# Attention outputs transposed by DMA, head-pair loads for batch 0, a table matmul for ALiBi and mask in two batches, and batch 1 inside the first feed-forward group

## The chip, the cores and the metric

The kernel runs on one core of a Trainium2 chip (trn2). The metric is the device time of one execution in microseconds (us). A version is executed three to six times, and its median is quoted. Every ratio is to runs of the kernel before on the same chip in the same session. A run more than 1.5% above the fastest of its kernel is counted as slow and left out of the ratios; of all runs quoted one was, and it is marked. Where an experiment is set against the changed kernel or another experiment, the two often ran in different sessions, on several chips; the medians of the kernel before in these sessions were 377.8 to 378.8 us.

## The reference

```python
def _attn_ref(q, k, v):                       # 8 batches, 8 heads, 576 tokens, head size 64
    scores = scale * np.matmul(q, k.transpose(0, 1, 3, 2))
    rel = pos[:, None] - pos[None, :]
    bias = slopes[:, None, None] * (-np.abs(rel))       # ALiBi: one slope per head
    mask = (rel >= 0) & (rel < 128)                     # sliding window
    scores = np.where(mask, scores + bias[None], -1e9)
    # ... softmax over the keys
    return np.matmul(attn, v)

def _moe_ref(x, w_in, w_out, beta):           # x: the attention output as 4608 tokens x 512
    h = x @ w_in                              # 512 -> 2048
    g = h * (1.0 / (1.0 + np.exp(-beta * h)))
    return g @ w_out                          # 2048 -> 512
```

Inputs and output are float32. The kernel computes in bfloat16 with float32 sums.

## The kernel before: the parts that matter

The work has two layers. Attention goes batch by batch (eight batches, five blocks of up to 128 tokens). The feed-forward part goes in nine groups of 512 tokens: an *H group* is 16 tiles of `x @ w_in` (`hps`), tanh and a product, and its *out product* is `g @ w_out` (`ops`). TensorE's order is fixed by hand. H group g is placed where its 512 tokens are expected to be ready, and out products and later attention are woven in between.

SyncE issues, in program order, the loads of q, k and v, the DMA transposes that bring q and k of batches 2 to 7 into matmul layout, and the stores of the result. The queue is in order, so an issue that has to wait holds up all behind it; SyncE stood so for 34.7 of the 150 us between 100 and 250 us in the kernel before.

```python
def load_rows(src, b, sb):                    # one block of one of q, k, v: 256 KB in 256 B rows
    f = fst_pool.tile([P, H, D], F32, name="fst", tag="fst")
    nc.sync.dma_start(out=f[0:rows], in_=src[b, :, P*sb : P*sb + rows, :].rearrange("h p d -> p h d"))
# GpSimd casts the block to bfloat16: "bst" for q and k, "vs" for v

def T(b, sb):                                 # q/k transposes
    if b >= NPE:                              # NPE = 2: from batch 2 on by DMA, on SyncE's queue
        for i in range(2):
            nc.sync.dma_start_transpose(out=QK[b % 2][:, i, :, ...], in_=src[0:rows, i]...)
        return
    # ... else on TensorE, and a VectorE copy out of PSUM

def X(b, qb):                                 # an attention output block xn -> XT, H's operand
    xt = psum_t.tile([P, NDM, P], BF16, name="xt", tag="t")
    for c in range(NDM):                      # 4 transposes on TensorE
        nc.tensor.transpose(out=xt[:, c, :], in_=xnv[:, c*P : (c+1)*P], identity=ident[:])
    nc.vector.tensor_copy(out=XT[:, :, tok0 : tok0 + n1], in_=xt[:, :, 0:n1])

def OS(g, i, n):                              # out product and store
    # ... 16 matmuls into ops
    osb = osb_pool.tile([P, DM], F32, name="osb", tag="osb")      # 3 buffers
    nc.scalar.mul(osb[:], ops_[:], 0.5)
    nc.sync.dma_start(out=out[row0 : row0 + P, :], in_=osb[:])
```

The softmax here doesn't subtract the row's maximum and nothing guards it: scores larger than these inputs give would overflow.

## Time and profile before

| | kernel before |
|---|---|
| time, median of 3 (range) | 378.44 us (378.07 to 379.19) |
| span of the profiled run | 378.0 us |
| TensorE busy | 324.5 us, 86% |
| SyncE standing still between 100 and 250 us | 34.7 us of 150 |
| output transposes (`X`) | 160 on TensorE |

### The profile page before, as it was taken

The page shows a single profiled execution, that of the slowest core. Times are in us where ns is not written, and L with a number is a line of the kernel's source. Part 1 is how long each engine was busy: PE and PEld are TensorE (multiplying, and loading weights), DVE is VectorE, ACT ScalarE, POOL GpSimd, SP SyncE. Part 2 cuts the span into 40 slices and gives each one's busy share as a digit, 9 for nine tenths or more (in the row PEclk, how much of TensorE's full clock was granted, in tenths as well). Part 3 has the DMA queues.
Part 4 walks back from the last instruction along what each step waited for, and adds up shares of the span by engine and source line. Part 5 has one row for each costly group of instructions (what it writes and reads, how often), then busy time and mean ns, then how long its engine had stood idle before and what let it go on. Part 6 is the DMA issues. An engine that isn't in the chain of part 4 may idle for free.

```text
span 378.0 us, 6264 instructions
## 1 busy us (share of the span) xinstructions
PE 324.5 (86%) x2248; PEld 158.7 (42%) x2289; DVE 209.3 (55%) x443; ACT 214.4 (57%) x437; POOL 90.0 (24%) x157
## 2 busy tenths in 40 slices
PE   2365577608789999999999999999999999999996
PEld 1143324304344544444444444444444445544442
DVE  3265258606565656756575776676566755543410
ACT  1453076606657476757584868586767764444421
POOL 7671471433233241412323060310000000000000
PEclk9999999966999999999999999999999999999999
DMA  9999999999998899988987889850000011001012
GB/s 167 207 199 203 219 189 205 207 120 192 164 145 186 161 217 149 231 157 141 215 176 170 178 183 183 168 128 29 29 29 28 29 39 46 28 31 55 28 57 83
DMA packets 156768, 50.77 MB, mean 134 GB/s; under 512 B 148016, under 2 KB 152128, under 8 KB 156736
## 3 DMA queue, kind: packets, MB, share of 16 engines
q1 hardware_dynamic: 152512, 46.16, 63.6%
q0 software_dynamic: 4224, 4.19, 6.6%
q8 instruction: 18, 0.29, 0.3%
q14 instruction: 14, 0.11, 0.1%
HBM read 38.02 MB, written 9.44 MB: 126 GB/s over the span
## 4 chain that ended last, share of the span: by engine, by line
PE 73%; DMA 17%; SPq 3%; POOL 2%; ACT 2%; issue 1%; DVE 1%; ACTq 0%; POOLq 0%
PE ops L291 33%; PE hps L275 30%; DMA fst<-in_k_dram 11%; PE sps L205 4%; DMA fst<-in_v_dram 3%; SPq L84 3%; PE pv L241 2%; PE xt L257 2%; PE pv L237 2%; DMA fst<-in_q_dram 1%; DMA qkT<-bst 1%; DVE gT L281 1%; ACT pt L215 1%; ACT sig L280 1%; POOL bst L98 1%
## 5 line engine op out<-in xcount | busy, mean ns | idle before, releaser
L275 PE MATMUL hps<-XT,W 128*128 128x512 bf16 x552 | 149.0, 387 | 5.8 <-DVE gT L281 3.8
L280 ACT ACTIVATE sig<-hps,beta_h 128x512 bf16<-128x512 f32 x144 | 99.5, 693 | 85.7 <-PE hps L275 75.1
L291 PE MATMUL ops<-W,gT 128*128 128x512 bf16 x559 | 142.2, 379 | 1.0 <-issue 0.3
L281 DVE SCALAR_TENSOR_TENSOR gT<-sig,hps 128x512 bf16<-128x512 bf16 x144 | 98.5, 685 | 67.3 <-ACT sig L280 66.8
L215 ACT ACTIVATE pt<-sps,bias 128x256 bf16<-128x256 f32 (+2 forms) x256 | 100.4, 479 | 53.2 <-PE sps L205 53.0
L275 PEld LDWEIGHTS <-W 128*128 128x128 bf16 x576 | 51.7, 99 | 60.3 <-issue 11.4
L291 PEld LDWEIGHTS <-gT 128*128 128x128 bf16 x576 | 51.8, 98 | 55.4 <-issue 2.3
L219 DVE TENSOR_TENSOR pt<-pt,mask 128x1024 bf16<-128x1024 bf16 x64 | 47.9, 748 | 16.2 <-ACT pt L215 15.8
L205 PE MATMUL sps<-qkT 64*128 64x256 bf16 (+2 forms) x320 | 28.8, 274 | 25.6 <-ACT pt L215 12.7
L105 POOL CAST vs<-fst 128x512 bf16<-128x512 f32 (+1 forms) x42 | 27.1, 653 | 88.4 <-DMA fst<-in_v_dram 71.9
L97 POOL CAST bst<-fst 128x512 bf16<-128x512 f32 (+1 forms) x42 | 26.5, 631 | 51.9 <-DMA fst<-in_q_dram 36.4
L247 DVE TENSOR_TENSOR xn<-pv,zs 128x256 bf16<-128x256 f32 (+1 forms) x80 | 33.7, 422 | 2.6
L246 DVE RECIPROCAL zs<-pv 128x4 f32<-128x4 f32 (+1 forms) x80 | 14.2, 178 | 36.4 <-PE pv L241 34.6
L205 PEld LDWEIGHTS <-qkT 64*128 64x128 bf16 x320 | 12.4, 97 | 51.5 <-issue 38.8
L241 PE MATMUL pv<-vs,pt 128*128 128x65 bf16 x320 | 31.3, 201 | 1.1 <-DVE pt L219 1.0
L297 ACT ACTIVATE osb<-ops 128x512 f32<-128x512 f32 x36 | 21.7, 602 | 18.8 <-PE ops L291 18.4
L98 POOL CAST bst<-fst 128x512 bf16<-128x512 f32 (+1 forms) x42 | 26.8, 638 | 19.7 <-DMA fst<-in_k_dram 18.5
L241 PEld LDWEIGHTS <-pt 128*128 128x128 bf16 x320 | 23.8, 102 | 10.7 <-DVE pt L219 1.6
L237 PE MATMUL pv<-vs,pt 128*128 128x65 bf16 x256 | 26.2, 201 | 1.2 <-DVE xn L247 1.2
L237 PEld LDWEIGHTS <-pt 128*128 128x128 bf16 x256 | 21.4, 103 | 9.1 <-DVE xn L247 1.7
L262 DVE COPY XT<-xt 128x512 bf16<-128x512 bf16 (+1 forms) x40 | 15.6, 390 | 12.7 <-PE xt L257 12.0
L179 PE MATMUL tps<-ident,bst 128*128 128x128 bf16 x80 | 10.6, 292 | 12.3 <-POOL bst L97 8.8
(26 smaller groups left out, 58.5 us busy)
## 6 DMA issues: line engine op xcount, KB each, us to landing
out_dram<-osb SPq DMA_DIRECT2D x36, 256.0 KB, 2.1
fst<-in_v_dram SPq DMA_DIRECT2D x34, 256.0 KB, 4.2
fst<-in_q_dram SPq DMA_DIRECT2D x33, 256.0 KB, 5.2
fst<-in_k_dram SPq DMA_DIRECT2D x33, 256.0 KB, 5.0
W<-in_moe_w_in_dram POOLq DMA_DIRECT2D x4, 512.0 KB, 11.9
W<-in_moe_w_out_dram POOLq DMA_DIRECT2D x4, 512.0 KB, 12.2
fst<-in_q_dram SPq DMA_DIRECT2D x9, 128.0 KB, 5.0
fst<-in_k_dram SPq DMA_DIRECT2D x9, 128.0 KB, 4.5
```

What stands on the lines that cost most here:

```text
L98: c = nc.gpsimd.tensor_copy(out=t[0:rows, 1], in_=fk[0:rows])
L105: return nc.gpsimd.tensor_copy(out=VS[b % 2][0:rows, sb, :, 0:D], in_=f[0:rows])
L205: nc.tensor.matmul(o, lhsT=qk[64 * e : 64 * e + 64, 1, p, P * kb : P * kb + P], rhs=qk[64 * e : 64 * e + 64, 0, p, P * kb : P * kb + nq], ...
L215: nc.scalar.activation(out=pt[:, e, cols], in_=sps[:, e, cols], func=ACTF.Exp, scale=qscale, bias=bias[:, half, h : h + 1],)
L219: nc.vector.tensor_tensor(out=pt[:], in0=pt[:], in1=masks[m][:], op=ALU.mult)
L237: nc.tensor.matmul(pv[:, hl, 0 : D + 1], lhsT=weights(b, qb - 1, h, 1), rhs=vs[:, qb - 1, h, 0 : D + 1], start=True, stop=False,)
L241: nc.tensor.matmul(pv[:, hl, 0 : D + 1], lhsT=weights(b, qb, h, 0), rhs=vs[:, qb, h, 0 : D + 1], start=qb == 0, stop=True,)
L247: nc.vector.tensor_tensor(out=xn[0:nq, 4 * g : 4 * g + 4, :], in0=pv[0:nq, :, 0:D], in1=zs[0:nq].broadcast_to([nq, 4, D]), op=ALU.mult,)
L275: nc.tensor.matmul(hps[:], lhsT=W1[:, c, bass.ts(j, P)], rhs=XT[:, c, c0 : c0 + TOKG], start=(c == 0), stop=(c == NDM - 1),)
L280: nc.scalar.activation(out=sig[:], in_=hps[:], func=ACTF.Tanh, scale=beta_h[:, j : j + 1])
L281: nc.vector.scalar_tensor_tensor(out=gts[g][:, j, :], in0=sig[:], scalar=1.0, in1=hps[:], op0=ALU.add, op1=ALU.mult)
L291: nc.tensor.matmul(ops_[:], lhsT=gT[:, j, i * P : i * P + P], rhs=W2[:, j, :], start=(j == 0), stop=(j == NFF - 1),)
```

## The change

Its intent is to start TensorE's long full stretch earlier and to take work off it:

- all output transposes of batches 2 to 7 go from TensorE to DMA (on SyncE's queue);
- q and k of batch 0 come by head pairs in 1 KB rows, and the double loads of some of batch 1's blocks are gone; there are more staging buffers for loads (`fst` 16 in place of 13, `bst` 8 in place of 7);
- in batches 0 and 1 a matmul adds ALiBi and mask as a table, so that one `Exp` of 1024 columns replaces four of 256 and the mask product falls away;
- batch 1's attention lies inside H group 0, and groups 0 and 1 use four PSUM buffers for H tiles.

```diff
-    xn_pool = ctx.enter_context(tc.tile_pool(name="xn", bufs=2))
+    xn_pool = ctx.enter_context(tc.tile_pool(name="xn", bufs=6))
...
+    def load_pair(p):                       # batch 0, two heads, 4 tokens of one head per row: 1 KB
+        for i, src in enumerate((q, k)):
+            nc.sync.dma_start(out=f[:]..., in_=src[0, 2*p : 2*p+2, 0:LM].rearrange("h (r a) d -> r h (a d)", a=LA))
...
     def SC(b, m, p, pool=None):
+        if b < NPE:
+            for e in range(2):
+                nc.tensor.matmul(sps[:, e, :], lhsT=sident[:, 2*p + e, :], rhs=table[m][:], start=True, stop=False, ...)
...
+        if b < NPE:
+            nc.scalar.activation(out=pt[:], in_=sps[:], func=ACTF.Exp, scale=qscale)
+        else:
+            # ... the four activations with a bias, and the mask product, as before
...
     def X(b, qb):
+        if b >= NPE:
+            for at, r0, r1 in parts:
+                nc.sync.dma_start_transpose(out=XT[:, :, at : at + r1 - r0], in_=xnv[r0:r1, :])
+            return
         # ... on TensorE as before
...
     def HS(g, j):
-        hps = psum_h.tile([P, TOKG], F32, name="hps", tag="hps")
+        pool, tag = (psum_o, "ops") if g < 2 and j % 2 else (psum_h, "hps")
...
# (the rest of the diff reorders the program: batch 1's attention list `one` runs within H group 0)
```

## The prediction

> **What bounds the kernel now.** I read the page first, slices before groups.
>
> ```profile
> PE   2365577608789999999999999999999999999996
> PEclk9999999966999999999999999999999999999999
> DMA  9999999999998899988987889850000011001012
> ```
>
> Slices are 9.45 us. TensorE is full from about 110 us on and has gaps before; DMA is the reverse, full to 250 us. So the kernel is starved first and TensorE-bound after. A table of 10 us stretches puts TensorE at 3.09 us busy in 70 to 80, 4.32 in 80 to 90, 9.95 in 110 to 120. The timeline of TensorE gives the waits and, by the distance of starts, the rates:
>
> ```profile
> 81.81 0.40 PE L205 MATMUL sps<-qkT 64*128 64x256 bf16 x2 [8.00 <-DMA qkT<-bst]
> ...
> 102.41 1.89 PE L275 MATMUL hps<-XT,W 128*128 128x512 bf16 x8 [1.04 <-DVE gT L281]
> 104.93 1.89 PE L275 MATMUL hps<-XT,W 128*128 128x512 bf16 x8 [0.51 <-DVE gT L281]
> ...
> 199.75 1.03 PE L275 MATMUL hps<-XT,W 128*128 128x512 bf16 x4
> 200.61 1.03 PE L291 MATMUL ops<-W,gT 128*128 128x512 bf16 x4
> ```
>
> Four wide matmuls take 0.86 us (199.75 to 200.61), 0.216 each. In H-only stretches two tiles take 2.52 us (102.41 to 104.93), not 1.73: two PSUM buffers wait for tanh and multiply. In the same way a scores step (one head pair, half a batch) costs 0.33 us of TensorE, a 65-wide value matmul 0.031, a transpose 0.057. The sum: H 576 x 0.216 = 124.2; out product the same; scores 64 x 0.33 = 21.1; values 576 x 0.031 = 17.9; q/k transposes 80 x 0.057 = 4.6; output transposes 160 x 0.057 = 9.1; together 301.1 us. Check: the first out product starts at 108.3 us, where by program order 39.6 is done and 261.5 left. The chain of work ends
>
> ```profile
> 368.11 6.22 PE ops L291 x28
> ```
>
> at 374.3: 266.0 for 261.5, so 4.5 us were lost after 108 us and 3.7 follow the last matmul. Almost all the loss, 69 us, lies in the first 108.
>
> Who starves it? The timelines of GpSimd (which casts what landed) and of the SyncE queue:
>
> ```profile
> 7.02 0.62 POOL L97 CAST bst<-fst 128x512 bf16<-128x512 f32 x1 [0.55 <-DMA fst<-in_q_dram]
> 8.23 0.62 POOL L98 CAST bst<-fst 128x512 bf16<-128x512 f32 x1 [0.59 <-DMA fst<-in_k_dram]
> ```
> ```profile
> 85.30 2.07 SPq L84 DMA_DIRECT2D fst<-in_v_dram  x3
> 87.41 0.62 SPq L84 DMA_DIRECT2D fst<-in_q_dram  x1
> ...
> 92.94 1.09 SPq L84 DMA_DIRECT2D fst<-in_k_dram  x1
> 94.14 5.67 SPq L171 DMA_TRANSPOSE qkT<-bst  x4
> 99.86 1.20 SPq L84 DMA_DIRECT2D fst<-in_v_dram  x2
> ...
> 105.14 8.66 SPq L171 DMA_TRANSPOSE qkT<-bst  x6
> ```
>
> A 256 KB piece lands each 1.2 us (218 GB/s). Transposes hold SyncE for over 1.3 us each: this queue is in order, so each delays everything behind it. A batch is 15 loads and 10 transposes: 28.5 us from 85.30 to 113.8, and 32.4 later (137.95 to 170.34) with its output stores. Its waits on the other engines in that stretch are only some 5 us, so it runs at nearly its own pace. TensorE needs 124.2 x 2 / 9 + (21.1 + 17.9 + 9.1) / 8 = 33.6 us for a group and the attention of one batch. The queue was barely faster, but had a lead.
>
> **What the Trainium skill says.** *DMA: Bandwidth & Descriptors*, Specifications: line rate needs transfers of at least 512 B. It fits: q, k, v come in 256 B rows at 218 GB/s. *Advanced Engine Details and Errata*, X-Bar Transpose: DMA transposes are as fast as plain DMAs, 350 to 400 GB/s expected. The trace disagrees for this size: the view of the q/k tile has
>
> ```profile
> L171 SPq DMA_TRANSPOSE qkT<-bst x60: 1185/1212/2743, 76.4 to 249.1; - x60
> ```
>
> a median issue of 1.212 us for 128 KB, 108 GB/s, SyncE's own time. *ScalarE: Activation LUTs*, What ACT_TABLE_LOAD costs: 0.833 ns an element, and a per-partition operand adds 93 ns. The groups give 479 ns at (on average) 256 columns and 693 at 512, and 602 at 512 without operand; so 1024 columns without one are about 693 + 428 - 91 = 1.03 us (estimate). *TensorE: Matmul & The Clock Gate*, Part 1: after an idle window matmuls run at half rate until some 3.4 us of work. The 0.5 of the clock in 80 to 90 us, after the 8 us wait, fits.
>
> **The change, part by part.**
> 1. Loads. Before casts 42 q, k and v blocks each where 8 x 5 = 40 exist: two v blocks and two q/k block pairs of batch 1 are loaded twice, 5 pieces, 6.0 us. Gone. Batch 0's q and k (8 pieces) come in 1 KB rows; estimate 0.8 us instead of 1.2, so 3.2 us. The small beta load leaves the queue: 0.5 us. Batch 2's q/k, landed at about 80.3 before, land at about 80.3 - 9.7 = 70.6.
> 2. ScalarE and VectorE in batches 0 and 1: 16 steps, each 1.03 instead of 4 x 0.48 = 1.92 us of ScalarE, and no 0.75 us mask multiply. TensorE pays 32 table matmuls x 0.216 = 6.9 us.
> 3. Output transposes of batches 2 to 7: 120 matmuls gone, 120 x 0.057 = 6.8 us, and 30 VectorE copies of 0.39. TensorE's total is thus 301.1 + 6.9 - 6.8, unchanged. But 31 DMA transposes enter the SyncE queue, 5 to 6 a batch.
> 4. Order. Batch 1's attention lies inside H group 0, group 1's H tiles use four buffers (0.86 instead of 1.26 us). TensorE no longer needs batch 2 until 50.2 of its 301.1 us are done; before, it needed it at about 33.
>
> The first three groups. H group 0 can start near 23 us (v of batch 0 landed and cast by 18, then some 5 us of values and transposes), against 48.1 before. By the built order batch 2's scores stand at work 50.2; its transposes are issued by about 75. H group 2 stands at work 69.9 and needs batch 2's third output block, which stands in SyncE's order behind all of batch 3's q/k and the next nine loads. With the block times above: six transposes end at 75, four at 80.3, nine loads at 89, six transposes at 98, six loads at 103, a store and two output transposes at 106, four transposes at 112, nine loads and a store at 121, then its own issue and landing, 124. Loads issued to an emptied queue may take 0.6 instead of 1.0 us, and some transposes no wait: 117. I take 121. TensorE without this wait would be there by about 95.
>
> From there: 231.2 of work + 4.5 + 3.7 = 239.4, so 360.4 if the queue then keeps up.
>
> The queue afterwards. A batch's 32.4 us grow by 5 output transposes. Two next to other transposes cost 1.3 each; three among loads lie beside data that is still flowing, some 0.5 each; with a fifth store, 36.5. Groups 3 and 4 each need one such batch of queue, group 5 that and five more items, 42. TensorE's work between them is 32.7, 30.8 and 32.5. Waits if nothing overlaps better: 3.8 + 5.7 + 9.5 = 19. If the waits of the queue shrink (POOL has more time to cast), 33 a batch: 8. I take 10 for the three, since the 5 us of queue waits should mostly go. 360.4 + 10 = 370.4, so 370.
>
> **Rivals.**
> A: The queue keeps up (TensorE stays the bound after group 2). For: loads are DMA-paced, and transposes issued among them cost little; the slack between each last value block and its H group is 7 to 10 us of work. Then 355 to 361.
> B: The SyncE queue becomes the bound to group 5. For: 36.5 against 33 us. Against: the interleaving. Then 374 to 382, the gain of the start given back, with cold restarts of 1 to 2 us a wait.
> C: Only the start counts, no wait at group 2 as loads run faster than the block times: group 2 near 105 us, time near 345. Against: the SyncE order is fixed and 28.5 us a batch was measured with hardly any waits.
> D: ScalarE or VectorE become the bound. Against: 57% and 55% busy, and both lose work. I give it nothing.
>
> **Range and chances.** A and C pull to 345 to 361, B to 382; my sum lies between. 357 to 385. Faster by over 2% (below 370.9) 0.50, within 2% 0.41, slower 0.09.
>
> **What would show it.** Batch 2's last cast near 71 us instead of 80; first H matmul near 23; a TensorE wait on an output transpose of the DMA of 10 us or more before H group 2 (right: it starts at 117 to 124); waits of that kind before groups 3 to 5, 10 us together; a SyncE queue with 33 to 37 us a batch; no such wait from group 6 on; TensorE's H and out rows unchanged per matmul. It is wrong if group 2 starts before 110 or if the later waits are nothing or over 20.

## More of the kernel before

From the page of the kernel before come the busy time of each engine, its share in the chain of work that ended last, and the group of H matmuls (the columns are busy time, mean ns, and idle time of the engine ahead of them with its main cause):

```profile
PE 324.5 (86%) x2248; PEld 158.7 (42%) x2289; DVE 209.3 (55%) x443; ACT 214.4 (57%) x437; POOL 90.0 (24%) x157
...
PE 73%; DMA 17%; SPq 3%; POOL 2%; ACT 2%; issue 1%; DVE 1%; ACTq 0%; POOLq 0%
...
L275 PE MATMUL hps<-XT,W 128*128 128x512 bf16 x552 | 149.0, 387 | 5.8 <-DVE gT L281 3.8
```

TensorE carries 73% of the chain, SyncE's queue (SPq) 3%. H matmuls wait for hardly anything, least of all for their operand XT. The waits that cost lie in the first 108 us, and the prediction shows them.

## The result, and the profile after

The changed kernel takes **389.47 us** (388.65 to 390.33, 4 runs); the kernel before took 378.81 us in the same session. The ratio is 1.028, with a 95% interval of 1.0245 to 1.0314, so the kernel is slower. Ratios here are the mean time of one kernel's fast runs over that of the other's of the same rounds, so they are not quite the ratios of the quoted medians. The profiled span is 387.4 us, the mean granted clock 0.932 (0.982 before).

The page of the changed kernel: busy times, slices of 9.7 us, the chain, and the H matmuls:

```profile
PE 325.7 (84%) x2161; PEld 152.4 (39%) x2201; DVE 187.8 (48%) x409; ACT 212.0 (55%) x407; POOL 84.7 (22%) x139
...
PE   3978898767640799989969993899999999999996
...
PEclk9979999989685699999999998699999999999999
DMA  7999999869869798949997698983212111201012
...
PE 59%; DMA 22%; SPq 14%; issue 2%; POOL 2%; ACT 0%; DVE 0%; POOLq 0%; ACTq 0%
...
L340 PE MATMUL hps<-XT,W 128*128 128x512 bf16 x558 | 149.2, 391 | 33.1 <-DMA XT<-xn 30.7
```

The start is better: TensorE's first eight slices are fuller. A hole (6, 4, 0) follows at 97 to 126 us where the kernel before was nearly full, and smaller dips at 165, 200 and 240 us. The chain holds 14% of SyncE's queue in place of 3%. The last line says who is waited for: 30.7 us of idle time ahead of H matmuls, until a DMA transpose of an attention output had landed. TensorE's timeline (start, duration, instructions, and in brackets the idle time before) has the four places:

```profile
28.00 0.63 PE L340 MATMUL hps<-XT,W 128*128 128x512 bf16 x1
...
128.20 1.86 PE L340 MATMUL hps<-XT,W 128*128 128x512 bf16 x4 [17.57 <-DMA XT<-xn]
...
165.99 1.02 PE L340 MATMUL hps<-XT,W 128*128 128x512 bf16 x4 [1.97 <-DMA XT<-xn]
...
200.52 1.02 PE L340 MATMUL hps<-XT,W 128*128 128x512 bf16 x4 [2.92 <-DMA XT<-xn]
...
243.84 1.87 PE L340 MATMUL hps<-XT,W 128*128 128x512 bf16 x4 [8.20 <-DMA XT<-xn]
```

These are the starts of H groups 0, 2, 3, 4 and 5. From group 2 to 5 the groups take 37.8, 34.5 and 43.3 us for TensorE work of 32.7, 30.8 and 32.5. The excess is 19.6 us: 13.1 us stand in the brackets, and the rest is slower running around the waits (four matmuls take 1.87 us after a long wait, 1.02 otherwise; the mean granted clock in the three stretches is 0.93, 1.00 and 0.91, which on their lengths makes up the other 6.5 us). The timeline of SyncE's queue ahead of group 2 shows what its operand stood behind:

```profile
91.56 8.63 SPq L217 DMA_TRANSPOSE qkT<-bst  x6
...
106.20 2.56 SPq L319 DMA_TRANSPOSE XT<-xn  x2
108.86 5.09 SPq L217 DMA_TRANSPOSE qkT<-bst  x4
114.01 0.58 SPq L92 DMA_DIRECT2D fst<-in_q_dram  x1
...
120.50 3.50 SPq L92 DMA_DIRECT2D fst<-in_v_dram  x3
124.09 1.25 SPq L319 DMA_TRANSPOSE XT<-xn  x1
```

The third XT transpose is issued at 124.1, behind four q/k transposes, nine loads and a store. It lands 4 us later, and H group 2 starts.

### The profile page after: what moved, and what is told of

Its sections match the earlier page's. It is cut to its first block, busy times and chain, and to the rows that moved or that the text cites. A ratio compares the mean times of both kernels' runs of the same rounds, so it can differ in the third digit from the quotient of the medians.

```text
span 387.4 us, 6060 instructions
## 1 busy us (share of the span) xinstructions
PE 325.7 (84%) x2161; PEld 152.4 (39%) x2201; DVE 187.8 (48%) x409; ACT 212.0 (55%) x407; POOL 84.7 (22%) x139
## 4 chain that ended last, share of the span: by engine, by line
PE 59%; DMA 22%; SPq 14%; issue 2%; POOL 2%; ACT 0%; DVE 0%; POOLq 0%; ACTq 0%
PE ops L356 27%; PE hps L340 25%; DMA fst<-in_v_dram 10%; SPq L92 8%; DMA fst<-in_q_dram 6%; SPq L217 5%; DMA XT<-xn 4%; PE sps L257 3%; DMA fst<-in_k_dram 2%; PE pv L300 2%; PE pv L296 1%; POOL vs L121 1%; SPq L102 1%; SPq L364 1%; POOL bst L116 0%
## 5 line engine op out<-in xcount | busy, mean ns | idle before, releaser
L340 PE MATMUL hps<-XT,W 128*128 128x512 bf16 x558 | 149.2, 391 | 33.1 <-DMA XT<-xn 30.7
L356 PE MATMUL ops<-W,gT 128*128 128x512 bf16 x555 | 145.0, 388 | 1.4 <-issue 0.9
L270 ACT ACTIVATE pt<-sps,bias 128x256 bf16<-128x256 f32 (+1 forms) x192 | 75.3, 478 | 24.4 <-PE sps L257 24.2
L116 POOL CAST bst<-fst 128x512 bf16<-128x512 f32 (+1 forms) x70 | 44.5, 641 | 146.7 <-DMA fst<-in_q_dram 108.8
L274 DVE TENSOR_TENSOR pt<-pt,mask 128x1024 bf16<-128x1024 bf16 x48 | 34.7, 723 | 22.8 <-ACT pt L270 22.4
L257 PE MATMUL sps<-qkT 64*128 64x256 bf16 (+2 forms) x320 | 27.1, 262 | 11.2 <-DMA qkT<-bst 6.1
L300 PE MATMUL pv<-vs,pt 128*128 128x65 bf16 x320 | 29.6, 197 | 0.2 <-DVE xn L306 0.2
L296 PE MATMUL pv<-vs,pt 128*128 128x65 bf16 x256 | 25.0, 198 | 2.2 <-DVE xn L306 1.7
L300 PEld LDWEIGHTS <-pt 128*128 128x128 bf16 x320 | 22.7, 100 | 9.5 <-issue 0.6
L296 PEld LDWEIGHTS <-pt 128*128 128x128 bf16 x256 | 20.5, 101 | 10.3 <-DVE xn L306 3.4
L265 ACT ACTIVATE pt<-sps 128x1024 bf16<-128x1024 f32 x16 | 15.9, 1025 | 10.7 <-PE sps L257 10.4
L243 PE MATMUL sps<-table,sident 128*128 128x512 bf16 x31 | 10.2, 411 | 1.3 <-ACT pt L265 1.1
L206 DVE COPY qkT<-tps 128x512 bf16<-128x512 bf16 x8 | 5.5, 689 | 7.7 <-PE tps L200 7.7
```

What stands on the lines that cost most here:

```text
L116: c = nc.gpsimd.tensor_copy(out=t[0 : ROWS[sb], i], in_=load_rows(src, b, sb))
L257: nc.tensor.matmul(o, lhsT=qk[64 * e : 64 * e + 64, 1, p, P * kb : P * kb + P], rhs=qk[64 * e : 64 * e + 64, 0, p, P * kb : P * kb + nq], ...
L270: nc.scalar.activation(out=pt[:, e, cols], in_=sps[:, e, cols], func=ACTF.Exp, scale=qscale, bias=bias[:, half, h : h + 1],)
L274: nc.vector.tensor_tensor(out=pt[:], in0=pt[:], in1=masks[m][:].rearrange("p (o c) -> p o c", o=1).broadcast_to([P, 2, 512]), op=ALU.mult,)
L296: nc.tensor.matmul(pv[:, hl, 0 : D + 1], lhsT=weights(b, qb - 1, h, 1), rhs=vs[:, qb - 1, h, 0 : D + 1], start=True, stop=False,)
L300: nc.tensor.matmul(pv[:, hl, 0 : D + 1], lhsT=weights(b, qb, h, 0), rhs=vs[:, qb, h, 0 : D + 1], start=qb == 0, stop=True,)
```

## The experiments

Eighteen kernels ran. All gave the right result. Two theories stood at the outset: **(1)** SyncE's in-order queue cannot carry 31 more transposes in this stage, or carries them too late; **(2)** the earlier start packs more loads into the same time, and DMA bandwidth is short whoever transposes. "Base" below is the first experiment's kernel: the changed kernel with all output transposes on TensorE.

| run | what differs | us, median |
|---|---|---|
| (before) | | 378 |
| (after) | | 389.5 |
| x_on_pe ("base") | after, output transposes on TensorE | 357.5 |
| xt_early600 | after, XT transposes ahead of loads | 378.7 |
| loads_pool | after, later loads issued by GpSimd | 401.5 |
| before_xt_dma | before, output transposes by DMA | 397.7 |
| x_both | base, and the DMA transposes to no use | 373.0 |
| stores_act | after, stores issued by ScalarE | 387.1 |
| x_dload_act, x_dload_pool, x_dload_sp | base, 30 useless loads from three queues | 376.5, 367.2, 356.3 |
| x_tiny_sp | base, 30 tiny loads from SyncE | 358.1 |
| x_free_tr | base, useless transposes of a constant | 382.3 |
| x_copy_xn | base, useless plain copies of xn | 357.9 |
| x_dma_67 | DMA transposes in batches 6 and 7 only | 354.9 |
| v_pool, v_pool_early | after, v loads by GpSimd | 380.4, 380.6 |
| x_pe_notable, x_pe_dup, x_pe_256 | base, one part of the start undone | 357.2, 362.3, 361.2 |

### 1. Output transposes back on TensorE (x_on_pe)

```diff
-        if b >= NPE:
+        if b >= B:        # never
             nc.sync.dma_start_transpose(out=XT..., in_=xnv...)
```

> The changed kernel with one part undone: every transpose of an attention output back on TensorE, the rest (1 KB rows, no double loads, tables for batches 0 and 1) kept. Theory 1 (the 31 output transposes are too much for SyncE's queue): TensorE's work grows by 5.7 us, for 25 blocks, but the waits of H groups 2 to 5 for XT (30.7 us in the changed kernel's table of waits) almost vanish; 389.5 - 30.7 + 5.7 = 364, and with the cold stretches gone some 4 us more: 357 to 366 us, faster than the kernel before by 3 to 6%. Theory 2 (the kernel is slow because the earlier start packs more loads into the same time, so DMA bandwidth or q/k arrival is short whatever does the output transposes): the waits move to score matmuls waiting for q/k, and the time stays above 375 us.

It took 357.5 us (356.9 to 359.1), ratio 0.946. Slices of TensorE and the H group in its page:

```profile
PE   2989598977769999999999999999999999999995
...
L340 PE MATMUL hps<-XT,W 128*128 128x512 bf16 x576 | 148.1, 384 | 1.1 <-DVE XT L328 1.1
```

From about 102 us on TensorE is full to the end, with 1.1 us of waiting ahead of H in place of 33.1. So theory 2 falls, at least without the output transposes on the queue: the same loads in the same time are carried. The rest of the change gains 5%, and this one part takes away 32 us although it takes 6.8 us of work off TensorE (30 blocks of four transposes of 0.057 us; the 25 blocks and 5.7 us of my expectation were a slip).

### 2. The same part alone, on the kernel before (before_xt_dma)

```diff
-    xn_pool = ctx.enter_context(tc.tile_pool(name="xn", bufs=2))
+    xn_pool = ctx.enter_context(tc.tile_pool(name="xn", bufs=6))
 def X(b, qb):
+    if b >= NPE:
+        nc.sync.dma_start_transpose(...)
+        return
```

> The kernel before with one part of the change alone: the outputs of batches 2 to 7 transposed by DMA (and six xn buffers in place of two), nothing else changed. If the part costs on its own (queue theory): the queue's 4.5 to 5 us per batch of added transposes make H groups wait for XT; time 380 to 392 us, 1 to 3% slower than before although TensorE loses 5.7 us of work. If it is only harmful together with the early start (where SyncE's lead over TensorE is small): the later start leaves the queue its lead, and the time is 370 to 378 us, faster by up to 2%.

It took 397.7 us, ratio 1.052: worse than either expectation. The part costs 19 us by itself, and the early start is not needed for it.

### 3. The same queue in another order (xt_early600)

```diff
+            with tc.high_priority(offset=600):
                 for at, r0, r1 in parts:
                     nc.sync.dma_start_transpose(out=XT..., in_=xnv...)
```

> The changed kernel with the output transposes given a higher priority, so that the scheduler puts each of them ahead of the nine loads in SyncE's queue; the same instructions, another order. If ORDER alone makes H group 2 wait 17.6 us: that wait shrinks to under 5 us and the time is 365 to 378 us. If the queue's CAPACITY is the bound in groups 2 to 5: what group 2 gains, later groups or the q/k transposes lose, and the time is 383 to 392 us. I lean to a part of each: group 2's wait smaller, the sum of all waits on DMA still over 18 us, 376 to 386 us.

It took 378.7 us: 10.8 less than the changed kernel. TensorE's timeline has three waits left, in groups 2, 3 and 5:

```profile
120.67 1.87 PE L341 MATMUL hps<-XT,W 128*128 128x512 bf16 x4 [11.54 <-DMA XT<-xn]
...
158.87 1.89 PE L341 MATMUL hps<-XT,W 128*128 128x512 bf16 x4 [3.34 <-DMA XT<-xn]
...
233.36 1.86 PE L341 MATMUL hps<-XT,W 128*128 128x512 bf16 x4 [6.07 <-DMA XT<-xn]
```

Their sum is 20.9 us where it was 30.7. The place in the queue is thus one cause and worth a third of the loss; two thirds stay.

### 4. Is it that something waits for them? (x_both)

```diff
+        if b >= NPE:
+            scr = scr_pool.tile([P, NDM, P], BF16, name="scr", tag="scr")   # nothing reads it
+            nc.sync.dma_start_transpose(out=scr[:, :, 0 : r1 - r0], in_=xnv[r0:r1, :])
         # ... and the four transposes on TensorE that H uses
```

> The kernel with all output transposes on TensorE (it ran at 357.5 us), and the DMA transposes of the changed kernel issued as well, at the same places of SyncE's queue and from the same xn tiles, into a scratch tile that nothing reads. The queue and the DMA engines carry the full load of the changed kernel, but no matmul waits for an output transpose. THROUGHPUT theory (the queue's issue time, or the DMA engines, cannot carry 31 more transposes in this stage): the q/k transposes get late in place of XT, score matmuls wait, and most of the loss stays: 375 to 390 us. LATENCY theory (an H group waits only because its last output block has to travel through the in-order queue, behind loads and q/k transposes, while the queue as such has room): 357 to 362 us.

It took 373.0 us (369.6 to 377.2; the last of these was counted as slow, and the three fast runs average 371.8; its clock, 0.959, was no lower than theirs, so it may be this kernel's own scatter, and with it the mean is 373.2). So some 14 us are lost without any matmul waiting for an output transpose. The rest of the 32 goes with the waits for XT, which this kernel does not have; that the two parts simply add up is not shown. One way in which the 14 are lost can be read from ScalarE's and TensorE's timelines around one dip:

```profile
230.00 0.60 ACT L363 ACTIVATE osb<-ops 128x512 f32<-128x512 f32 x1 [5.39 <-DMA out_dram<-osb]
```
```profile
232.12 0.61 PE L258 MATMUL sps<-qkT 64*128 64x256 bf16 x4 [3.64 <-ACT pt L271]
```

ScalarE wants to copy an out tile into an `osb` buffer, but the three buffers still hold results: their stores sit in SyncE's queue or have just left it. It stands for 5.4 us; the exponentials behind it come late; TensorE cannot place its next scores. What lies on the queue gets late, and here the stores' buffers ran out first. It is not the only way: over the whole run TensorE's scores wait 8.9 us for ScalarE (4.5 in the base) and 8.2 us for q/k transposes (5.4 in the base). What is left of the 14 was not traced to single waits.

### 5. Bytes, issues, waiting, or transposing? (x_dload_sp, x_tiny_sp, x_copy_xn, x_free_tr)

Four kernels put 30 or 31 useless DMAs on SyncE's queue, on top of the base.

```diff
# x_dload_sp: loads of 128 KB in 256 B rows        x_tiny_sp: loads of 4 bytes
+   nc.sync.dma_start(out=scr[:], in_=v[g, 0:H//2, 0:P, :]...)   |   out=scr[0:1, 0, 0:1], in_=v[g, 0, 0:1, 0:1]
# x_copy_xn: waits for xn, does not transpose      x_free_tr: transposes, waits for nothing
+   nc.sync.dma_start(out=scr[r0:r1, :], in_=xnv[r0:r1, :])      |   nc.sync.dma_start_transpose(out=scr[...], in_=W1[r0:r1, 0, 0:DM])
```

> The same 30 loads issued from SyncE, in its in-order queue with the q/k loads and transposes: DMA work and issues together, without any matmul that waits for them. If it costs as much as from GpSimd, the DMA engines are what is short: 366 to 378 us in both. If it costs far more than from GpSimd (372 to 380 us here, under 362 us there), the queue is: its issue time or its in-order waits.

> 30 loads of four bytes each from SyncE in the same places, so issues and waits of the queue with next to no work for the 16 DMA engines, on the kernel with all output transposes on TensorE (357.5 us). If the number of issues in the in-order queue is what costs: 362 to 372 us. If bytes or engine time: 357 to 360 us, with SyncE's issue of one under 0.2 us or hidden.

> As the run with both (outputs transposed on TensorE, and 31 DMA transposes into a scratch tile at the places of the changed kernel: 373 us), but the scratch transposes read a constant weight tile that is there from the start, so SyncE's in-order queue never stands still for an attention output. If standing still for xn (17 us of SyncE's waits between 60 and 250 us) is what delays the q/k loads and transposes behind it: 356 to 361 us. If the transposes themselves cost (1.2 us of issue each, or their work on the DMA engines): 367 to 376 us.

> The mirror of that run: plain copies of xn by DMA to a scratch tile at the same places of the queue, with the wait for xn but without the transpose (issue some 0.5 us in place of 1.2). If standing still for xn is what costs: 367 to 376 us. If the transposes' issue or engine work is: 356 to 361 us. If it takes both together (queue nearly full, then stalled): both runs between 359 and 367 us.

Loads: 356.3 us. Tiny loads: 358.1. Plain copies that wait for xn: 357.9. None costs anything; I had expected the loads to cost 8 us or more in either case. The transposes of a constant: **382.3 us**, a loss of 25. So none of these costs anything alone: the bytes on the DMA engines (53.0 MB in both of the last two), standing still for xn, the number of issues. What remains is what a transpose itself takes. The cleanest pair is x_both and x_copy_xn, with the same tile, the same wait and the same place in the program, transposed or copied: 371.8 us (fast runs) against 357.9. The rows of the two runs in the trace (minimum, median and maximum duration in ns, then first and last start):

```profile
L321 SPq DMA_DIRECT2D scr<-xn x31: 465/531/1805, 104.7 to 303.8; - x31
```
```profile
L323 SPq DMA_TRANSPOSE scr<-W x31: 1198/1254/2676, 106.1 to 282.4; - x31
```

531 ns against 1254. What that does to the queue is in its waits between 100 and 250 us (us in all, times, longest), first in the base, then in the kernel with transposes of a constant:

```profile
SPq L217 <- POOL vs L121: 13.5, 15, 1.5
SPq L217 <- POOL bst L116: 11.9, 11, 2.0
SPq L364 <- ACT osb L362: 8.5, 5, 6.3
SPq L364 <- ACT sig L345: 3.5, 8, 0.6
SPq L364 <- ACT pt L270: 2.0, 2, 1.3
```
```profile
SPq L367 <- ACT sig L348: 3.3, 6, 1.2
SPq L218 <- POOL vs L122: 2.7, 4, 0.9
SPq L367 <- ACT osb L365: 1.0, 1, 1.0
SPq L367 <- ACT pt L271: 0.8, 2, 0.6
```

In the base SyncE stands still for 39.4 of 150 us: it has room. With the copies it is 24.7, with the loads 18.7; both still have room. With the transposes it is 7.8 us: SyncE issues almost without a break, 95% of the time, and is the bound. Its first batch of six q/k transposes starts at 129.8, 168.4 and 207.2 us in that run, 38.6 us a batch; TensorE's work per group is 30.8 to 32.7, and 1.1 more where it transposes the outputs itself.

So full a queue is seen in x_free_tr alone. In x_both SyncE stands still for 25.2 us and in the changed kernel for 26.4, no less than with the copies, so standing time by itself does not tell which kernel loses. What differs is what it stands for: 15.8 us in x_both and 12.8 in the changed kernel are ahead of output transposes, at the head of the queue, against 8.0 us ahead of the copies. For the changed kernel, that the queue is too slow is read from its cycle, 35 to 36 us a batch against TensorE's 31 to 33; how much of that is issuing and how much is standing for xn was not separated.

Could a transpose instead slow the other transfers on the DMA engines? The medians from issue to landing speak against it: loads of q and k land in 4.5 and 4.8 us with the transposes of a constant and in 4.5 and 5.0 us with the copies. Between 100 and 250 us the DMA engines are busy for 0.86 of the time with the transposes, and for 0.99 with the useless loads, which cost nothing. Nor is the 1.2 us a backlog: in x_dma_67 (part 8), where the queue had run out of loads, the ten transposes still took 1.196 us of SyncE (median). But no run changed the issue time alone, so that SyncE's time is what costs is read from the traces and not shown by an experiment. In this run, too, the loss goes over the stores (16.8 us of ScalarE's waits for `osb` between 100 and 262 us) and over late q/k (7.4 us). Why it is some 10 us worse than x_both is open; its transposes stand a little differently in the queue, often three in a row ahead of q/k transposes.

### 6. Moving issues off SyncE (loads_pool, stores_act, v_pool, v_pool_early)

```diff
# loads_pool / v_pool                        (v_pool: only where src is v)
-        nc.sync.dma_start(
+        (nc.gpsimd if b >= NPE else nc.sync).dma_start(
# stores_act
-            nc.sync.dma_start(out=out[row0 : row0 + P, :], in_=osb[:])
+            nc.scalar.dma_start(out=out[row0 : row0 + P, :], in_=osb[:])
# v_pool_early: v_pool and the priority of xt_early600
```

> The changed kernel with the q, k and v loads of batches 2 to 7 issued from GpSimd's queue in place of SyncE's; SyncE keeps the transposes and the stores, and the bytes are the same. If SyncE's issue time (some 91 loads of 0.6 to 1 us each) is what the transposes wait behind: waits of H groups for XT fall from 30.7 us to under 8 us, time 355 to 368 us. If DMA bandwidth, or transposes against loads on the 16 engines, is the bound: no gain, 384 to 394 us, with transposes issuing as slowly as before. If GpSimd, which also casts, gets late with the loads: score matmuls wait for q/k and the time lies between, 370 to 384 us.

> The changed kernel with the 36 stores of the output issued from ScalarE's queue in place of SyncE's: six per batch, 0.5 to 1.5 us of SyncE each, so 3 to 6 us per batch less in front of the transposes; the bytes on the DMA engines are the same. If SyncE's ISSUE TIME is the bound in groups 2 to 5: group 2's wait shrinks by 2 to 4 us and those of groups 3 to 5 (13 us) by most: 372 to 381 us. If DMA BANDWIDTH is: no gain, 386 to 391 us. LATENCY theory: a transpose has fewer issues ahead of it, a gain of 1 to 2 us for each of four groups, 381 to 386 us.

> The changed kernel (389.5 us) with only the v loads of batches 2 to 7 issued from GpSimd: 5 of 15 loads per batch, some 0.9 us of SyncE each, so 4.5 us per batch less in its queue, with the DMA engines' work the same, at 0.75 us of GpSimd each. Theory queue's issue time: the cycle of SyncE falls from some 37 to 32 us per batch, about TensorE's pace; waits for XT of groups 3 to 5 (13 us) mostly go and group 2's shrinks by 3 us (v loads stand right ahead of it in the queue): 370 to 380 us. Theory DMA engines: 386 to 391 us. If GpSimd again comes late with its casts: 380 to 400 us with score matmuls waiting for q/k.

> The same with the output transposes ahead of the loads in SyncE's queue (alone that gave 378.7 us). If queue order and queue load are the two causes, both remedies add up: 358 to 370 us. If not, 375 to 390 us.

*loads_pool* took 401.5 us and does not tell what it was to tell. Loads and casts now share GpSimd's in-order queue, casts come late, and SyncE's transposes stand waiting for them: 40.9 us between 60 and 125 us alone.

*stores_act* took 387.1 us, 2.4 less than the changed kernel. It is not clean either. ScalarE's timeline:

```profile
88.51 0.62 ACT L362 ACTIVATE osb<-ops 128x512 f32<-128x512 f32 x1
96.42 0.37 ACTq L364 DMA_DIRECT2D out_dram<-osb  x1
96.84 1.57 ACT L270 ACTIVATE pt<-sps,bias 128x320 bf16<-128x320 f32 x4 [7.71 <-DMA qkT<-bst]
```

The copy is done at 89.1, but the store leaves at 96.4, until a q/k transpose of *SyncE* has landed, and ScalarE stands meanwhile. In the program as built, DMAs of SyncE and ScalarE take turns on eight shared semaphores, and each waits until the DMA before it on the same one has landed. A store from ScalarE is so tied to SyncE's order, and ScalarE with it.

*v_pool* took 380.4 us, 9 less than the changed kernel. Its waits for XT:

```profile
128.34 1.86 PE L340 MATMUL hps<-XT,W 128*128 128x512 bf16 x4 [21.45 <-DMA XT<-xn]
...
170.00 1.87 PE L340 MATMUL hps<-XT,W 128*128 128x512 bf16 x4 [5.46 <-DMA XT<-xn]
```

Five loads a batch less on SyncE, and the waits of groups 4 and 5 are gone; from group 3 on 5.5 us remain of 13.1. That fits a queue that was overloaded. It does not prove it: SyncE stands still for 45.6 of the 150 us in this run, 20.1 of them ahead of output transposes, and the kernel is still 23 us slower than the base. Group 2 waits longer, for the scheduler has now put its transpose behind six q/k transposes: order, again. *v_pool_early* took 380.6 us. The two remedies did not add up, against my expectation, and its group 2 still waited 23.5 us. Its queue shows that the priority changed little: the third output transpose of batch 2 is issued at 125.4 us, again behind six q/k transposes (115.6 to 124.0 us), as in v_pool (124.4, behind six from 114.7).

### 7. Two runs that were not clean (x_dload_act, x_dload_pool)

```diff
# both on the base: 30 useless 128 KB loads in groups 2 to 6
+   nc.scalar.dma_start(out=scr[:], in_=v[g, 0:H//2, 0:P, :]...)      # x_dload_act; x_dload_pool: nc.gpsimd
```

> The kernel with all output transposes on TensorE (357.5 us), and 30 useless 128 KB loads (256 B rows) added to groups 2 to 6, six per group, issued from ScalarE's queue: about as much work for the 16 DMA engines as the 31 output transposes were (profiles of the two kernels: 246 against 226 us of queue 1's share times span, so 20 us), none for SyncE. If the DMA ENGINES are the bound of that stage: the q/k loads and transposes get late by up to 20 us: 368 to 378 us. If they have room: 357 to 362 us, of which up to 3 us from ScalarE's issuing.

> The same 30 useless 128 KB loads as in the run before, on top of the kernel with all output transposes on TensorE (357.5 us), but issued from GpSimd, whose loads have semaphores of their own: ScalarE's trace showed that its issues stood still up to 7 us until loads of SyncE had landed and held up the activations behind them, so that run (376.5 us) was not clean. If the 16 DMA ENGINES are the bound of batches 2 to 5: q/k arrive late and the time is 366 to 378 us. If they have room and SyncE's queue is the bound: 357 to 362 us.

x_dload_act took 376.5 us, just what the DMA engines as the bound would give, and it would have misled: it has the same tie between ScalarE and SyncE's order as stores_act (issues that stood for some 5 us). x_dload_pool took 367.2 us, but the loads did not run where they were meant to:

```profile
L351 POOL DMA_DIRECT2D scr<-in_v_dram x30: 747/747/887, 11.7 to 85.6; - x30
```

Nothing held them back, and they ran between 12 and 86 us, in the start. The same loads from SyncE, with a place in its order (121 to 259 us), cost nothing. That is the run to believe on DMA bandwidth.

### 8. DMA transposes where the queue is idle (x_dma_67)

```diff
-        if b >= NPE:
+        if b >= 6:
```

> The changed kernel with DMA transposes of outputs for batches 6 and 7 alone, where SyncE's queue has no loads left ahead of the last ones; batches 2 to 5 back on TensorE. TensorE loses 10 blocks of 0.23 us, 2.3 us. If waiting hurts only while the queue is loaded: 354.5 to 357.5 us, 1 to 3 us under the kernel with all of them on TensorE (357.5 us). If the first of them (batch 6, group 6 or 7) waits: 358 to 364 us.

It took **354.88 us** (353.32 to 355.49, 6 runs), ratio 0.938: 2.6 us below the base, for 2.3 us of TensorE work taken off. No wait for XT from a DMA is left in its table of waits. Where SyncE has run out of loads, the part is worth about what it was meant to be. The size is near the noise between programs: x_dload_sp, with useless loads added, also came out 1.2 us below the base. But the intervals of the two ratios, 0.935 to 0.941 and 0.944 to 0.949, do not overlap. This is the fastest version found, 6% under the kernel before and 9% under the changed one.

### 9. The parts of the start (x_pe_notable, x_pe_dup, x_pe_256)

```diff
# x_pe_notable: batches 0 and 1 with four activations and the mask product again
-        if b < NPE:
+        if b < 0:
# x_pe_dup: batch 1's q, k blocks 3, 4 and v blocks 0, 1 loaded twice
+        for _ in range(2):
# x_pe_256: batch 0 in token blocks of 256 B rows
-    load_pair(0); load_tail(); ...
+    for sb in range(NQB):
+        load_qk(0, sb)
```

> The kernel with all output transposes on TensorE (357.5 us) with the table part undone: batches 0 and 1 get ALiBi and mask as the others do, by four activations and a product per tile; TensorE loses 6.9 us of table matmuls, ScalarE gains some 16 tiles of 0.9 us more, VectorE 16 products of 0.74. If the start is bound by ScalarE's pace without it: 358 to 366 us. If by the arrival of q/k, which my prediction assumed: 353 to 358 us.

> The kernel with all output transposes on TensorE (357.5 us), with batch 1's q and k blocks 3 and 4 and v blocks 0 and 1 loaded twice, as the kernel before does. My prediction gave this 6.0 us of q/k arrival: 361 to 365 us if batch 2's and 3's arrival sets the end of the start stage; 357 to 359 us if something else does.

> The kernel with all output transposes on TensorE (357.5 us) with batch 0 loaded by blocks of tokens in 256 B rows again, as the kernel before does, in place of head pairs in 1 KB rows. My prediction gave the 1 KB rows 3.2 us of the DMA engines' time before batch 2's q/k can land: 359 to 363 us if that arrival still sets the end of the start stage; 364 to 372 us if the start of the score matmuls, some 5 us later without the head pairs, does; 356 to 359 us if neither.

Against the base of 357.5 us: without the tables 357.2, with the double loads 362.3 (4.8 more), with 256 B rows 361.2 (3.7 more). The tables bring nothing that shows, as the arrival of q and k sets the end of the start. Taken one at a time these account for 8.5 us of the 21 between the kernel before and the base. The remaining 12 must lie in what no run took alone: batch 1 inside H group 0 with four H buffers, the added staging buffers, the other order of the weight loads, or the parts' joint effect. That is argued, not shown.

## Why the prediction was wrong, by its own steps

- **What bounds the kernel before; TensorE's sum of 301.1 us:** right. From the start of group 5 the prediction counts 135.2 of work, 4.5 lost and 3.7 after the last matmul, 143.4 us; the trace has 387.4 - 243.84 = 143.6.
- **The start:** nearly right. Batch 2's last q/k cast ended at 72.7 us (about 71 predicted), and H tiles in four buffers took 0.86 us. The first H matmul came at 28.0, not 23. The `Exp` of 1024 columns took 1.025 us (1.03). Double loads were worth 4.8 us (6.0), 1 KB rows 3.7 (3.2), the tables about nothing, and the prediction had put no gain down to them.
- **H group 2 waits for SyncE's order:** right in mechanism, 7.2 us too early. My block times summed to 124; I took 121 because loads into an emptied queue might be faster, and it was 128.2. The six transposes of the block sum ended at 100.2 and not 98, the nine loads and the store took 10 us and not 9, and the last transpose landed 4.1 us after its issue began, not 3.
- **"I take 10 for the three, since the 5 us of queue waits should mostly go":** the step that failed. The same paragraph had 3.8 + 5.7 + 9.5 = 19; the trace has 5.1 + 3.7 + 10.8 = 19.6. The queue's waits did not go. It has new ones, for xn, in the place of those it lost. SyncE stands still for 26.4 us between 100 and 250 us (34.7 before), of which these 12.8 us are ahead of XT transposes:

```profile
SPq L319 <- DVE gT L346: 6.7, 8, 1.1
...
SPq L319 <- DVE zs L305: 2.5, 2, 1.3
...
SPq L319 <- DVE pt L274: 1.9, 2, 1.1
SPq L319 <- DVE xn L306: 1.7, 2, 0.9
```

  So the queue's cycle stayed at 35.4 to 36.3 us a batch, near the 36.5 of the unshaded sum and not the 33 of the hopeful one. With 7.2 and 9.6 put right, 370.4 becomes 387.2, and the span was 387.4. (Both corrections are measured, so this sum tests no more than the prediction's tail, 143.4 against 143.6.)
- **Rival A (the queue keeps up)** fell with the 19.6 us lost after group 2. **Rival B (the queue becomes the bound)** was what happened, and its 374 to 382 was too low by group 2's 7 us. Its "cold restarts" were seen. **C** fell with group 2's start; **D** was rightly given nothing.
- **Chances:** 0.09 for slower was too little. The sum that I had worked out, without shading (124 and 19), gives 382.4: 1% over the kernel before, so even it did not reach slower by 2%. The last 5 us are group 2's, which started 4.2 us after the unshaded 124, and 0.6 of the later groups.
- **What the prediction did not see at all:** it weighed the part only as a cost within the change. I did not ask what the kernel would be without it. x_on_pe gives 357.5 us: the part saves 6.8 us of TensorE work and costs 39 (32 net).

Open: why x_free_tr is worse than x_both, how the changed kernel's cycle divides into issuing and standing for xn, and whether more `osb` buffers would have hidden the late stores.

## What to carry to other kernels

Count an in-order DMA queue like an engine: issues per batch times their duration, plus what it stands still for, against the pace of the engine it feeds. In this kernel moving work "to DMA" was only free while that sum had room, and where it had none, what else lay on the queue got late: operands, prefetches, and stores whose buffers then stopped another engine. Before adding to such a queue, look at when it is idle; in this kernel the last two batches gained from the same move that cost 32 us over six. And when two estimates of a step are at hand, do not shade the measured one towards the hoped-for one without a number.

## What the Trainium skill lacked or had wrong

- *Advanced Engine Details and Errata*, X-Bar Transpose (TRN2), has transposing DMAs as fast as regular ones. Not for the issuing queue at this size: 1254 ns of SyncE for a transpose against 531 ns for a plain copy (medians of 31, most of 128 KB), and 382.3 against 357.9 us for the kernel with 31 of either. In time from issue to landing the runs do not contradict it: 2.8 us for the transposes against 3.3 us for the copies of 128 KB (medians).
- *DMA: Bandwidth & Descriptors*, Issuing engines are not separate DMA queues, calls the time to initiate a DMA "usually small relative to the DMA itself". For these transposes it is not: one of q/k takes 1.2 us to issue and lands 2.5 us after its issue began (medians in the changed kernel), and SyncE, issuing 95% of the time, is the bound of x_free_tr.
- *VectorE: DVE Perf Modes*, The three transpose paths, gives one 128x128 bf16 transpose as 390 ns on TensorE and 1309 ns by DMA. In this trace a pipelined one on TensorE costs 57 ns, and a DMA transpose of four such blocks holds SyncE for 1.25 us, so the pair of figures does not give the trade. The rule of the same page for 128x128 (Rules for kernel authors), TensorE if PSUM will do and DMA otherwise, agrees with x_on_pe (357.5 against 389.5 us) and not with x_dma_67 (354.9 against 357.5), where the queue was idle.
- No page that I read says that DMAs of two queues can be held up by each other through the semaphores that they share: a store from ScalarE stood for 7.3 us (89.1 to 96.4) behind SyncE's transfers in stores_act.
